# Values and phi(keys) turned by VectorE blocks and two DMA hops instead of TensorE transposes

## The chip, the cores and the metric

The kernel runs on one core of a Trainium2 chip. A core has five engines that run side by side: TensorE (PE in the profile; PEld is its weight load), VectorE (DVE), ScalarE (ACT), GpSimd (POOL) and SyncE (SP), which here issues most DMAs. Each engine takes its instructions in order and waits on semaphores for the others. The metric is device time in microseconds, the median of several runs.

## The reference: attention with a compressive memory, then an MLP

Input x is 2048 tokens by 1024. The first block normalises the rows, projects them to queries, keys and values of 32 heads of 32, and works in four segments of 512 tokens. Each segment has softmax attention inside it and a read of a memory M that earlier segments have written:

```python
phi = lambda t: jnp.where(t > 0, t + 1.0, jnp.exp(t))
for s in range(N):
    qs, ks, vs = q[:, :, s], k[:, :, s], v[:, :, s]
    p = _softmax(einsum("bhqd,bhkd->bhqk", qs, ks) * scale + mask)
    a_dot = einsum("bhqk,bhkd->bhqd", p, vs)
    num = einsum("bhld,bhde->bhle", phi(qs), M)
    den = einsum("bhld,bhd->bhl", phi(qs), z)[..., None] + 1e-6
    outs.append(g * num / den + (1.0 - g) * a_dot)
    M = M + einsum("bhld,bhle->bhde", phi(ks), vs)
    z = z + einsum("bhld->bhd", phi(ks))
```

The result is projected by wo and added to x; a layer norm, a dense layer to 3584, GELU and a dense layer back to 1024 follow, with a second residual. Everything is float32.

## The kernel before, in words

Float32 accuracy comes from splitting each factor into an upper half of the reduced type fp32r and the remainder, and from three products (upper by upper, upper by lower, lower by upper). `mm3` (L114 to L117) issues such a triple. The upper half is a copy, mostly by ScalarE, and the lower half a subtraction, by VectorE or GpSimd.

The tokens are worked in two halves of 1024. A half runs attention over two segments, then the output projection (`wo_first`, `wo_second`), then the MLP, whose two matrix products are built from shared partial sums. Only attention is touched.

Attention works in units. A unit is a group g of four heads (128 columns, eight groups) and one segment s of 512 tokens; a half has 16 units, the kernel 32. Two generators run interleaved, one step of each in turn, 24 steps a unit (counted over a unit, steps 0 to 7 project keys, 8 to 15 queries, 16 to 23 values):

- `dense` (L402) projects keys, queries and values of the unit, eight steps each (`kps`, `qps`, `vps`: 128 x 512 in PSUM, columns of the heads on the partitions, tokens along the row). The keys' and queries' halves are copied by SP into stacks `ks` and `qs` of 96 partitions (`stack`, 12 DMAs of 64 KB for each; five buffers, so a stack waits until the logits of an earlier head are done).
- `heads` runs softmax attention of the four heads of the unit before, one head per six steps, as a pipeline over three heads (`slot`, the list PLAN): logits `pqk`, exponential on ScalarE, normalisation `pr` on GpSimd (L557), transposes `ppt` of the weights on TensorE (L573), halves `pth` and `ptl`, products `po` with the values (L593).

Two tensors have to be turned, so that tokens lie on the partitions: the values, for `po` and for the memory update, and phi(keys) (`pk`, L369) for the memory update. phi(keys) is turned in segments 0 to 2 (24 units), the values in all 32.

- phi(keys): in step 1 of the value projection TensorE makes four transposes `pkn` (L453), ScalarE copies the upper half `pkh` (L455), and one step later VectorE subtracts for `pkl` (L457).
- Values: after the projection ScalarE copies `vps` to `vt` (L461). The generator `late` (L466) belongs to a unit but runs behind the next unit's steps, from step 2 of its key projection on. It begins with four transposes `vn` (L469) and the two halves of `vs` (L471, L472).

Then `late` lists small products, which go one by one into the places where `one_small` is called (before each `ppt` and most `po`): the memory read, 12 products `pm`, and the memory update, 12 products `pmm`, which need `vs`, `pkh` and `pkl`. The update of the state `MZ` follows (L497 on VectorE, L499 to L502 on GpSimd), and the next segment's unit copies its halves `mzh`, `mzl` on GpSimd in step 20 of its own. `pom` turns the memory output back (L516).

PSUM has three banks of the kind `d` (`ps_dense`), which projections, `pkn`, `vn`, `pm`, `pmm` and `pom` share. Within attention a scheduler fixes each engine's order before the run; the engines then follow that order whatever the real times are. The weights of the next group come as three DMAs `wr` of 512 KB (L326) and are split into `wh` and `wl` (L92).

Of the kernel before, what the change touches and what calls it, by code (L numbers as in the profile page):

```python
# [10 lines left out]
F32 = mybir.dt.float32  # L11
# [28 lines left out]
def raw(ap):  # L40
    return ap.bitcast(F32)


def build(tc, x, wq, wk, wv, wo, beta, w1, b1, w2, b2, out):
# [6 lines left out]
    def ps_dense(name):  # L51
        return psum.tile([P, 512], F32, tag="d", name=name, bufs=3)
# [29 lines left out]
    p1_dram = [dram.tile([P, 512], F32, name=f"p1_dram{j}") for j in range(FB // 2)]  # L82
    h_dram = [[dram.tile([S // P, P, FB // 4, P], F32, name=f"h_dram{i}{s}") for s in range(2)] for i in range(2)]

    acts = {}

    def split(pool, w, hi, lo, hi_eng="vector", lo_eng="gpsimd"):
# [256 lines left out]
    def attention(half, first):  # L344
# [4 lines left out]
        def tmp(name):  # L349
            return ab.tile([P, 512], F32, tag="tmp", name=name, bufs=5)  # L350

        def tmpr(name):
            return ab.tile([P, 512], F32R, tag="tmpr", name=name, bufs=6)

# [47 lines left out]
        def dense(g, sl, ws, u):  # L402
# [15 lines left out]
            for c in project(ws["q"], sl, "qps", qps):  # L418
                if c == 0:
                    u["ks"] = stack(kh, kl, "ks", (0, 1, 0))  # L420
                if c == 2 and s < 3:
                    zc = ab.tile([P, 64], F32, name="zc", bufs=2)[:, 0:1]
                    pk = phi_sum(kparts, "pk", zc)
                next(behind, None)
                yield
            qh, ql = tmpr("qh"), tmpr("ql")
# [6 lines left out]
            for c in project(ws["v"], sl, "vps", vps):  # L433
                if c == 0:
                    u["qs"] = stack(qh, ql, "qs", (0, 0, 1))
                if s > 0:
                    if c == 2:
                        pq = phi_sum(qparts, "pq")
                    if c == 4:
                        while small:  # L440
                            one_small()
                        pqh, pql = tmpr("pqh"), tmpr("pql")
                        mzh = ab.tile([P, 256], F32R, name="mzh", bufs=1)[:, 0:132]
                        mzl = ab.tile([P, 256], F32R, name="mzl", bufs=1)[:, 0:132]
                        nc.scalar.copy(pqh, pq)
                        nc.gpsimd.tensor_copy(mzh, MZ[:, g, :])
                        nc.gpsimd.tensor_tensor(mzl, MZ[:, g, :], raw(mzh), op=ALU.subtract)
                    if c == 5:
                        nc.gpsimd.tensor_tensor(pql, pq, raw(pqh), op=ALU.subtract)
                if c == 1 and s < 3:  # L450
                    pkn = ps_dense("pkn")
                    for i in range(4):
                        nc.tensor.transpose(pkn[:, i * P:(i + 1) * P], pk[:, i * P:(i + 1) * P], ident)  # L453
                    pkh, pkl = tmpr("pkh"), tmpr("pkl")
                    nc.scalar.copy(pkh, pkn)  # L455
                if c == 2 and s < 3:
                    nc.vector.tensor_tensor(pkl, pkn, raw(pkh), op=ALU.subtract)  # L457
                next(behind, None)
                yield
            vt = tmp("vt")  # L460
            nc.scalar.copy(vt, vps)  # L461
            vs = ab.tile([P, 16, 64], F32R, name="vs", bufs=2)
            u["vs"] = vs
            omt = u["omt"] = tmp("omt") if s > 0 else None

            def late():  # L466
                vn = ps_dense("vn")
                for c in range(4):
                    nc.tensor.transpose(vn[:, c * P:(c + 1) * P], vt[:, c * P:(c + 1) * P], ident)  # L469
                vn3 = vn.rearrange("p (a b) -> p a b", b=DH)  # L470
                nc.scalar.copy(vs[:, :, 0:32], vn3)  # L471
                nc.vector.tensor_tensor(vs[:, :, 32:64], vn3, raw(vs[:, :, 0:32]), op=ALU.subtract)  # L472
                yield
                if s > 0:
                    om = tmp("om")

                    def memory(i2, ps):
                        pm = ps.rearrange("p (a b) -> p a b", a=2)
                        rg = ab.tile([P, 2, 32], F32, name="rg", bufs=2)[:, :, 0:4]
                        nc.vector.scalar_tensor_tensor(  # L480
                            rg, pm[:, :, 128:132], DEN_EPS, bb[:, 4 * g:4 * g + 4].unsqueeze(1).to_broadcast([P, 2, 4]),
                            op0=ALU.add, op1=ALU.mult)
                        nc.vector.reciprocal(rg, rg)
                        nc.vector.tensor_tensor(
                            om[:, i2 * 256:(i2 + 1) * 256].rearrange("p (a h e) -> p a h e", a=2, h=4),
                            pm[:, :, 0:128].rearrange("p a (h e) -> p a h e", h=4),
                            rg.unsqueeze(3).to_broadcast([P, 2, 4, DH]), op=ALU.mult)

                    for i2 in range(2):
                        smalls("pm", [(lambda ps, ii=ii: ps[:, 256 * ii:256 * ii + 132],  # L490
                                       pqh[:, (2 * i2 + ii) * P:(2 * i2 + ii + 1) * P],
                                       pql[:, (2 * i2 + ii) * P:(2 * i2 + ii + 1) * P], mzh, mzl, True, True)
                                      for ii in range(2)], partial(memory, i2))
                left = len(small)
                if s < 3:
                    def update(pmm):
                        nc.vector.tensor_tensor(MZ[:, g, 0:P], pmm[:, 0:P], MZ[:, g, 0:P], op=ALU.add)  # L497
                        own = MZ[:, g, 0:P].rearrange("p (h e) -> p h e", h=4)
                        nc.gpsimd.tensor_tensor(own, own, hsel.unsqueeze(2).to_broadcast([P, 4, DH]), op=ALU.mult)  # L499
                        z = ZC[:, g:g + 1]  # L500
                        nc.gpsimd.tensor_scalar(z, z, zc, None, op0=ALU.add)
                        nc.gpsimd.tensor_scalar(MZ[:, g, 128:132], hsel, z, None, op0=ALU.mult)  # L502

                    smalls("pmm", [(lambda ps: ps[:, 0:P].rearrange("p (a b) -> p a b", a=4),
                                    pkh[:, c * P:(c + 1) * P], pkl[:, c * P:(c + 1) * P],
                                    vs[:, 4 * c:4 * c + 4, 0:32], vs[:, 4 * c:4 * c + 4, 32:64], c == 0, c == 3)
                                   for c in range(4)], update)
                total = len(small)
                while len(small) > total - left:
# [72 lines left out]
        def av(st, n):  # L582
# [3 lines left out]
            po = st["po"]  # L586
            for jk in (0, 1) if n == 0 else (3, 2):
                w = 512 - P * jk
                v = u["vs"][:, 4 * jk + j, :]
                for part in ("pth", "ptl"):  # L590
                    if (jk, part) != (3, "ptl"):
                        one_small()
                    nc.tensor.matmul(po[:, P * jk:], v, st[part][:, koff[jk]:koff[jk] + w],  # L593
                                     start=(jk, part) == (0, "pth"), stop=(jk, part) == (2, "ptl"))
# [849 lines left out]
```

## Time and profile before

| what | value |
|---|---|
| median of 3 runs | 2300.75 us (2300.48 to 2301.89) |
| the profiled execution: first to last instruction | 2296.2 us |
| between that span and the median | 4.55 us |
| instructions in the profile | 35279 |
| DMA in the profile | 355.36 MB, 155 GB/s on average |
| attention, half 0 | up to about 500 us |
| attention, half 1 | about 920 to 1380 us |

In the profile's rows a duration of a matmul includes its way through the array, so that rows overlap: the distance between starts tells what one costs. A row of a tile's view gives the line, engine, operation, the tiles, the count, and the shortest, median and longest duration. A timeline row gives the start in us, the duration in us, the engine, the line, the operation, the tile it writes and those it reads. SPq rows are SP issuing a DMA; a row of DMA issues ends with the median us from issue to landing.

### The profile page before, as it was taken

How to read it: one execution, taken by the hardware profiler on the slowest of the kernel's cores; microseconds unless marked ns; L12 is line 12 of the kernel's file. 1: busy time of each engine (PE TensorE's matmuls, PEld its weight loads, DVE VectorE, ACT ScalarE, POOL GpSimd, SP SyncE). 2: the span in 40 equal slices, each digit the busy share in tenths (PEclk: the TensorE clock that was granted, in tenths of full speed). 3: DMA queues.
4: the chain of work that ended last, by engine and by line, in shares of the span. 5: the costliest groups of instructions: out<-in, count | busy, mean ns of one | idle time of the engine just before them, and what ended most of it. 6: DMA issues, size and time to landing. Idle time of an engine off the chain costs nothing.

```text
span 2296.2 us, 35279 instructions
## 1 busy us (share of the span) xinstructions
PE 2270.4 (99%) x11769; PEld 1890.8 (82%) x11769; DVE 1540.3 (67%) x3173; ACT 1225.0 (53%) x2549; POOL 1092.4 (48%) x1134
## 2 busy tenths in 40 slices
PE   8999999999999999999999999999999999999999
PEld 6888888878888888888888887888888888888887
DVE  6777777776655565777777777565566766577563
ACT  6777777775453445777777776363344223322221
POOL 5545555555244442555555556253445554155430
PEclk9999999999999999999999999999999999999999
DMA  6333333345465654433333344466667976476762
GB/s 190 92 85 91 93 89 85 87 120 182 139 204 172 188 165 142 113 91 86 85 87 88 87 111 140 156 211 175 176 188 263 345 243 216 159 253 221 249 234 90
DMA packets 322719, 355.36 MB, mean 155 GB/s; under 512 B 26190, under 2 KB 218730, under 8 KB 322538
## 3 DMA queue, kind: packets, MB, share of 16 engines
q1 hardware_dynamic: 259370, 316.40, 45.4%
q10 hardware_dynamic: 63168, 36.71, 5.3%
q8 instruction: 93, 1.52, 0.3%
q14 instruction: 88, 0.72, 0.1%
HBM read 226.59 MB, written 76.09 MB: 132 GB/s over the span
## 4 chain that ended last, share of the span: by engine, by line
PE 91%; ACT 3%; POOL 2%; DVE 2%; issue 1%; DMA 1%; ACTq 0%; SPq 0%; POOLq 0%; DVEq 0%
PE po L1278 22%; PE bps L882 9%; PE cps L882 7%; PE dps L882 6%; PE po L593 6%; PE ppt L573 6%; PE pqk L541 3%; PE vps L116 2%; PE vps L115 2%; PE kps L115 2%; PE kps L116 2%; PE vps L117 2%; PE kps L117 2%; PE pwo L117 2%; PE pwo L116 2%; PE pwo L115 2%
## 5 line engine op out<-in xcount | busy, mean ns | idle before, releaser
L557 POOL TENSOR_SCALAR pr<-pr,nm,gate 128x128 f32<-128x128 f32 (+3 forms) x512 | 322.6, 639 | 345.9 <-DVE nm L554 260.0
L550 ACT ACTIVATE pr<-pr,mx 128x256 f32<-128x256 f32 (+3 forms) x512 | 287.6, 562 | 161.9 <-DVE mx L542 158.2
L580 DVE TENSOR_TENSOR ptl<-ppt,pth 128x512 fp32r<-128x512 f32 (+1 forms) x384 | 227.2, 599 | 86.2 <-ACT pth L575 82.0
L542 DVE CUSTOM_DVE_ANT_0 pr<-pqk,mask 128x256 f32<-128x256 f32 (+3 forms) x512 | 243.3, 484 | 46.5 <-PE pqk L541 43.7
L573 PE MATMUL ppt<-ident,pr 128*128 128x128 f32 x1280 | 223.6, 277 | 2.1 <-POOL pr L557 1.4
L575 ACT CAST pth<-ppt 128x512 fp32r<-128x512 f32 (+1 forms) x384 | 194.2, 517 | 39.0 <-PE ppt L573 33.1
L1288 DVE TENSOR_TENSOR c<-c,po 128x512 f32<-128x512 f32 x160 | 105.4, 683 | 143.1 <-PE po L1278 135.5
L573 PEld LDWEIGHTS ppt<-ident,pr 128*128 128x128 f32 x1280 | 164.6, 140 | 32.5 <-POOL pr L557 2.6
L541 PE MATMUL pqk<-ks,qs 96*128 96x256 f32 (+3 forms) x512 | 161.3, 315 | 0.0
L92 POOL TENSOR_TENSOR wl<-wr,wh 128x1024 fp32r<-128x1024 f32 x52 | 124.5, 2393 | 70.8 <-PE pqk L541 27.6
L593 PE MATMUL po<-pth,vs 128*64 128x512 f32 (+3 forms) x512 | 155.4, 326 | 0.3 <-ACT pth L575 0.2
L593 PE MATMUL po<-ptl,vs 128*64 128x512 f32 (+3 forms) x512 | 153.9, 310 | 1.3 <-DVE ptl L580 1.2
L1278 PE MATMUL po<-w2h,zh 128*128 128x512 f32 x378 | 121.1, 390 | 0.8 <-DVE zh L1218 0.4
L1135 POOL TENSOR_TENSOR w2r<-w2r 128x512 f32<-128x512 f32 x54 | 85.4, 1593 | 72.0 <-DVE c L1288 36.9
L541 PEld LDWEIGHTS pqk<-ks,qs 96*128 96x128 f32 x512 | 96.2, 188 | 21.5
L994 POOL TENSOR_TENSOR s<-r 128x512 f32<-128x512 f32 x28 | 43.6, 1559 | 143.4 <-DVE sa L1010 87.1
L882 PE MATMUL bps<-zh,sb 128*128 128x512 f32 x336 | 111.0, 391 | 0.0
L882 PE MATMUL bps<-zh,sa 128*128 128x512 f32 x336 | 110.8, 390 | 0.0
L115 PE MATMUL vps<-yh,wh 128*128 128x512 f32 x256 | 109.4, 427 | 0.9 <-DVE MZ L497 0.9
L115 PE MATMUL kps<-yh,wh 128*128 128x512 f32 (+1 forms) x264 | 110.1, 417 | 0.0
L115 PE MATMUL qps<-yh,wh 128*128 128x512 f32 x256 | 106.8, 417 | 0.0
L1278 PE MATMUL po<-w2h,hl 128*128 128x512 f32 x322 | 103.2, 390 | 0.5 <-POOL hl L1218 0.3
(241 smaller groups left out, 6657.1 us busy)
## 6 DMA issues: line engine op xcount, KB each, us to landing
hr<-h_dram SPq DMA_DIRECT2D x112, 448.0 KB, 5.4
w2r<-in_B_w SPq DMA_DIRECT2D x122, 256.0 KB, 4.4
r<-in_B_w SPq DMA_DIRECT2D x56, 512.0 KB, 4.5
h_dram<-ht ACTq DMA_DIRECT2D x84, 256.0 KB, 3.7
ks<-kh SPq DMA_DIRECT2D x256, 64.0 KB, 2.0
qs<-qh SPq DMA_DIRECT2D x256, 64.0 KB, 2.0
wr<-in_A_wo SPq DMA_DIRECT2D x32, 512.0 KB, 4.0
wx<-in_B_w SPq DMA_DIRECT2D x56, 256.0 KB, 3.5
```

Of the source, the lines that this page charges most:

```text
L115: nc.tensor.matmul(ps, ah, bh, start=first, stop=False)
L116: nc.tensor.matmul(ps, ah, bl, start=False, stop=False)
L541: nc.tensor.matmul(pqk[:, :n], u["qs"][j][:, i * P:(i + 1) * P], u["ks"][j][:, 0:n], start=True, stop=True)
L542: nc.vector.tensor_tensor_reduce(out=st["pr"][:, offs[i]:offs[i] + n], in0=pqk[:, :n], in1=mask[:, 512 - n:512], op0=ALU.add, op1=ALU.min, ...
L550: nc.scalar.activation(pi, pi, AF.Exp, bias=mx[:, i:i + 1], scale=-1.0, accum_out=mx[:, 4 + i:5 + i])
L557: nc.gpsimd.tensor_scalar(pi, pi, nm[:, 4 + k:5 + k], gate[:, 1, 4 * g + j:4 * g + j + 1], op0=ALU.mult, op1=ALU.mult)
L573: nc.tensor.transpose(ppt[:, o:o + P], pr[:, offs[i] + jk * P:offs[i] + (jk + 1) * P], ident)
L575: acts["pth"] = n, nc.scalar.copy(pth[:, base:base + w], ppt[:, :w])
L580: nc.vector.tensor_tensor(o, x0, x1, op=ALU.subtract)
L593: nc.tensor.matmul(po[:, P * jk:], v, st[part][:, koff[jk]:koff[jk] + w], start=(jk, part) == (0, "pth"), stop=(jk, part) == (2, "ptl"))
L882: nc.tensor.matmul(ps, x_[:, c, :], y_[:, c, :], start=first and c == 0 and n == 0, stop=last and c == 3 and n == 2, skip_group_check=True)
L1278: nc.tensor.matmul(ps, x_[:, k], y_[k], start=opens and k == 0 and i == 0, stop=closes and k == self.KP - 1 and i == 2, skip_group_check=True)
```

## The change

Neither tensor is turned by TensorE any more. A new function `turned` does it in two hops. VectorE transposes each 32 x 32 block of the 128 x 512 tile in place of its block (a single instruction; for the values it reads PSUM). SP stores the result to one of four scratch buffers in memory, and four loads, one for each quarter of the 128 target partitions, bring it back with the blocks in the places that a full transpose gives them, but for the order along the row: heads outermost, then the four blocks of 128 tokens. The later readers are rewritten for that order (`vk`, and `4 * j + jk` in `av`).

- phi(keys): `turned` is called in step 3 of the query projection, the copy to `pkh` moves from step 1 to step 2 of the value projection and reads SBUF, and the subtraction for `pkl` moves from VectorE in step 2 to GpSimd in step 3.
- Values: `turned` reads `vps` itself, so the copy `vt` goes. In `late` the memory products are listed first; the upper half of `vs` is made six steps later, the lower half one step after it, and the update products are listed two steps after that.
- The scratch tiles `scr` in SBUF take the place of two tiles that hold weights of the output projection after attention.

```diff
+    turn_dram = [dram.tile([P, 512], F32, name=f"turn_dram{k}") for k in range(4)]
...
+        scr = [acts["zt"].tile([P, 4, 512], F32, tag=f"t{x_}3", name=f"sc{x_}") for x_ in "hl"]
+
+        def turned(src, to, at):
+            mid = at
+            nc.vector.transpose(mid.rearrange("p (c k d) -> p c k d", c=4, k=4), src.rearrange("p (k c d) -> p c k d", c=4, k=4))
+            d = turn_dram[acts.get("turned", 0) % len(turn_dram)]
+            acts["turned"] = acts.get("turned", 0) + 1
+            nc.sync.dma_start(d, mid)
+            for c in range(4):
+                nc.sync.dma_start(to[32 * c:32 * c + 32].rearrange("j (h x) -> j h x", h=4),
+                                  d[:, c * P:(c + 1) * P].rearrange("(h j) x -> j h x", h=4))
...
+                if c == 3 and s < 3:
+                    kn = scr[1][:, 2 + sl]
+                    turned(pk, kn, scr[1][:, sl])
...
-                if c == 1 and s < 3:
-                    pkn = ps_dense("pkn")
-                    for i in range(4):
-                        nc.tensor.transpose(pkn[:, i * P:(i + 1) * P], pk[:, i * P:(i + 1) * P], ident)
+                if c == 2 and s < 3:
                     pkh, pkl = tmpr("pkh"), tmpr("pkl")
-                    nc.scalar.copy(pkh, pkn)
-                if c == 2 and s < 3:
-                    nc.vector.tensor_tensor(pkl, pkn, raw(pkh), op=ALU.subtract)
+                    pkn = kn.rearrange("p (h k d) -> p k h d", h=4, k=4)
+                    pk4 = [x_.rearrange("p (k h d) -> p k h d", h=4, k=4) for x_ in (pkh, pkl)]
+                    nc.scalar.copy(pk4[0], pkn)
+                if c == 3 and s < 3:
+                    nc.gpsimd.tensor_tensor(pk4[1], pkn, raw(pk4[0]), op=ALU.subtract)
...
-            vt = tmp("vt")
-            nc.scalar.copy(vt, vps)
+            vn = scr[0][:, 2 + sl]
+            turned(vps, vn, scr[0][:, sl])
...
             def late():
-                vn = ps_dense("vn")
-                for c in range(4):
-                    nc.tensor.transpose(vn[:, c * P:(c + 1) * P], vt[:, c * P:(c + 1) * P], ident)
-                vn3 = vn.rearrange("p (a b) -> p a b", b=DH)
-                nc.scalar.copy(vs[:, :, 0:32], vn3)
-                nc.vector.tensor_tensor(vs[:, :, 32:64], vn3, raw(vs[:, :, 0:32]), op=ALU.subtract)
-                yield
                 if s > 0:
...
+                for _ in range(6):
+                    yield
+                vn3 = vn.rearrange("p (a b) -> p a b", b=DH)
+                nc.scalar.copy(vs[:, :, 0:32], vn3)
+                yield
+                nc.vector.tensor_tensor(vs[:, :, 32:64], vn3, raw(vs[:, :, 0:32]), op=ALU.subtract)
+                vk = vs.rearrange("p (h k) e -> p k h e", h=4)
+                yield
+                yield
                 left = len(small)
...
-                                    vs[:, 4 * c:4 * c + 4, 0:32], vs[:, 4 * c:4 * c + 4, 32:64], c == 0, c == 3)
+                                    vk[:, c, :, 0:32], vk[:, c, :, 32:64], c == 0, c == 3)
...
-                v = u["vs"][:, 4 * jk + j, :]
+                v = u["vs"][:, 4 * j + jk, :]
```

## The prediction

> **What bounds the kernel now.** I read the engine totals first, then the chain that ended last, then the waits of TensorE, then the busy time of the two attention stages.
>
> ```profile
> span 2296.2 us, 35279 instructions
> PE 2270.4 (99%) x11769; PEld 1890.8 (82%) x11769; DVE 1540.3 (67%) x3173; ACT 1225.0 (53%) x2549; POOL 1092.4 (48%) x1134
> PE 91%; ACT 3%; POOL 2%; DVE 2%; issue 1%; DMA 1%; ACTq 0%; SPq 0%; POOLq 0%; DVEq 0%
> ```
> ```profile
> sum 915.00, PE 910.00 PEld 768.24 DVE 686.99 ACT 669.90 POOL 500.48; mean PE 455.00 PEld 384.12 DVE 343.49 ACT 334.95 POOL 250.24
> ```
> ```profile
> PE ppt L573 <- POOL pr L557: 1.4, 4, 0.5
> ```
>
> The chain is TensorE for 91% of the span. The second fence sums two stretches, 45 to 500 us and 920 to 1380 us, which are the attention of the two halves, the only place that the change touches: TensorE is busy for 910.0 of 915.0 us, VectorE for 75%, ScalarE 73%, GpSimd 55%. The last line is a row of TensorE's waits (total, times, longest): even its normalised weights `pr` are late only four times. So every microsecond of TensorE issue that goes is a microsecond of the result, until some other engine's chain becomes late.
>
> **The change, part by part.** What goes and what is replaced:
>
> ```profile
> L453 PE MATMUL pkn<-ident,pk x96: 270/272/273, 31.5 to 1333.3; 128*128 128x128 f32 x96
> L469 PE MATMUL vn<-ident,vt x128: 271/272/329, 40.6 to 1380.8; 128*128 128x128 f32 x128
> L457 DVE TENSOR_TENSOR pkl<-pkn,pkh x24: 678/680/691, 34.3 to 1335.4; 128x512 fp32r<-128x512 f32 x24
> ```
>
> 224 transposes leave TensorE: 24 groups of four for the keys, 32 for the values. Their 272 ns each are no measure, because they overlap; what counts is how far they push apart the starts around them.
>
> ```profile
> 209.73 0.39 PE L117 MATMUL qps<-yh,wl 128*128 128x512 f32 x1
> 209.96 0.34 PE L541 MATMUL pqk<-ks,qs 96*128 96x384 f32 x1
> 210.13 0.60 PE L573 MATMUL ppt<-ident,pr 128*128 128x128 f32 x4
> ...
> 213.46 0.39 PE L117 MATMUL vps<-yh,wl 128*128 128x512 f32 x1
> 213.69 0.60 PE L453 MATMUL pkn<-ident,pk 128*128 128x128 f32 x4
> ...
> 214.58 0.40 PE L116 MATMUL vps<-yl,wh 128*128 128x512 f32 x1
> ...
> 220.91 0.39 PE L117 MATMUL vps<-yh,wl 128*128 128x512 f32 x1
> 221.14 0.38 PE L573 MATMUL ppt<-ident,pr 128*128 128x128 f32 x2
> 221.28 0.48 PE L115 MATMUL kps<-yh,wh 128*128 128x512 f32 x1
> 221.60 0.39 PE L116 MATMUL kps<-yl,wh 128*128 128x512 f32 x1
> ...
> 224.21 0.39 PE L117 MATMUL kps<-yh,wl 128*128 128x512 f32 x1
> 224.44 0.60 PE L469 MATMUL vn<-ident,vt 128*128 128x128 f32 x4
> 224.79 0.43 PE L541 MATMUL pqk<-ks,qs 96*128 96x384 f32 x1
> 225.06 0.60 PE L573 MATMUL ppt<-ident,pr 128*128 128x128 f32 x4
> ...
> 251.19 0.48 PE L115 MATMUL kps<-yh,wh 128*128 128x512 f32 x1
> ```
>
> A unit (one head group, one segment) lasts 251.19 - 221.28 = 29.9 us, from its first key product to that of the next; it has 24 steps of about 1.25 us.
>
> - Values: from L117 over one pqk of 384 to ppt takes 225.06 - 224.21 = 0.85 us with `vn` in between, and 210.13 - 209.73 = 0.40 without. 0.45 us a group, 32 x 0.45 = 14.4 us.
> - Keys: from L117 over two ppt and L115 to L116 takes 214.58 - 213.46 = 1.12 us with `pkn`, 221.60 - 220.91 = 0.69 without. 0.43 us, 24 x 0.43 = 10.3 us.
>
> Together **-24.7 us** on the bounding engine. The Trainium skill, VectorE: DVE Perf Modes, The three transpose paths, gives 390 ns for one 128x128 on TensorE in bf16 and 311 ns for VectorE, which turns 32x32 blocks alone, and its Rules for kernel authors keep a 128x128 transpose on TensorE where PSUM will do; that rule speaks against this change. By its price TensorE would shed an estimated 224 x 0.39 = 87 us; these rows show 0.11 us of issue for each.
>
> Small products. The 12 update products `pmm` of a unit move from steps 4 to 8 into steps 11 to 14 of the next unit, behind the halves of the values; the memory products `pm` take their old places. In the built order of the changed kernel they stand among ppt and po as before. Four of them cost:
>
> ```profile
> 215.85 0.22 PE L541 MATMUL pqk<-ks,qs 96*128 96x128 f32 x1
> 216.71 0.39 PE L115 MATMUL vps<-yh,wh 128*128 128x512 f32 x1
> ...
> 227.25 0.39 PE L117 MATMUL kps<-yh,wl 128*128 128x512 f32 x1
> 228.16 0.48 PE L115 MATMUL kps<-yh,wh 128*128 128x512 f32 x1
> ...
> 230.80 0.22 PE L541 MATMUL pqk<-ks,qs 96*128 96x128 f32 x1
> 231.97 0.40 PE L115 MATMUL qps<-yh,wh 128*128 128x512 f32 x1
> ```
>
> Among transposes 0.91 us against the 0.58 (224.21 to 224.79) of a projection and four transposes alone: 0.08 each. Among four po 1.17 against 0.86: 0.08 each. The move is worth 0; with 288 of them and some 0.005 us of uncertainty, 1.5 us to either side.
>
> Other engines, a unit. ScalarE loses the copy `vt`. VectorE loses `pkl` (0.68) and gets two block transposes of 128x512, one from PSUM. No such operation is in the trace. The nearest row is the subtraction above at 0.68 us; half of it and twice of it are the bounds, and I take 0.7, since size and engine are the same: two of them less `pkl` are +0.7 us of 29.9, from 75% to some 78%, beside TensorE.
>
> The transfers are the real question. Each turn is one 256 KB store to memory and, after it has landed, four 64 KB loads, all issued by SP, in order, between the `ks`/`qs` copies.
>
> ```profile
> ks<-kh SPq DMA_DIRECT2D x256, 64.0 KB, 2.0
> wr<-in_A_wv SPq DMA_DIRECT2D x16, 512.0 KB, 4.4
> o_dram<-ot SPq DMA_DIRECT2D x28, 256.0 KB, 2.3
> ```
> ```profile
> 205.62 0.53 SPq L609 DMA_DIRECT2D o_dram<-ot  x1
> 212.04 0.51 SPq L377 DMA_DIRECT2D ks<-kh  x1
> ```
> ```profile
> 214.37 0.60 ACT L455 CAST pkh<-pkn 128x512 fp32r<-128x512 f32 x1
> 260.94 0.59 ACT L413 CAST kh<-kps 128x512 fp32r<-128x512 f32 x1 [1.14 <-PE kps L117]
> ```
> ```profile
> 255.50 0.37 SPq L326 DMA_DIRECT2D wr<-in_A_wq  x1
> ```
>
> A turn takes, from the store's issue: 2.3 us to land (as o_dram), four issues of 0.6 (0.51 to 0.53 in these rows, and a little between), 2.0 for the last to land: 2.3 + 2.4 + 2.0 = 6.7 us. Bounds: 5.5 us (2.0 + 3 x 0.51 + 2.0, both hops as quick as a `ks` copy) and 10.6 us (4.4 + 3 x 0.6 + 4.4, both hops as slow as the weight load `wr`). I take the middle one, since o_dram has the store's size and form and `ks` the loads' size.
>
> - Keys: in the built order the store stands behind o_dram, at 206.2 us on this unit's clock; it ends at 212.9. The consumer `pkh` is moved one step, from 214.37 to 214.9 at the earliest. 2.0 us of slack; SP is free from 206.2 to 212.04, so `ks` behind it loses up to 0.5 us, and those wait for a buffer anyway. At the bound of 10.6 us ScalarE stands 1.9 us, the exponentials queue behind `pkh`, `pkl` on GpSimd behind it, and `pr` behind that.
> - Values: the projection ends at 221.3, the block transpose some 1 us later, the store near 222.8, the loads land at 229.5. The consumer `vs` stands next to `kh`, 10 us behind the start of the unit, that is 231.3 or later. 1.8 us of slack. In a unit whose successor loads weights, SP puts two weight loads between store and loads; the second waits for GpSimd until 255.50, so the four loads go at 255.9 and land near 260.3, while `kh` is at 260.94. Slack 0.5 us, gone if anything slips.
>
> GpSimd in the units with weights is where I expect the first wait:
>
> ```profile
> 242.78 2.40 POOL L92 TENSOR_TENSOR wl<-wr,wh 128x1024 fp32r<-128x1024 f32 x1 [1.12 <-PE pqk L541]
> 245.16 1.42 POOL L557 TENSOR_SCALAR pr<-pr,nm,gate 128x384 f32<-128x384 f32 x2
> ```
> ```profile
> 247.50 0.60 PE L573 MATMUL ppt<-ident,pr 128*128 128x128 f32 x4
> ```
>
> GpSimd gets `pkl`: 1.2 us, half of what `wl` takes for twice the columns, 55% to 58% of a unit, between two `pr`. `pr` ends at 246.58, and ppt wants it at 247.50: 0.92 us. TensorE, with the key group gone, wants it 0.43 us sooner. The memory state's update, four operations of at most 132 columns (by the 1.42 us that two `pr` of 896 columns take, 0.3 each, 1.2 us), now falls just ahead of `wl`, because `pmm` ends in step 14 instead of step 8, and starts `wl` 0.2 to 0.5 us late. That uses up the slack: I take 0.2 us in the 16 units of this kind, 3 us, and 2 us more for the two ends of attention, where the scratch for the turned tiles is the home of two weight tiles of the output projection, which now wait for the last `vs`. **+5 us**, bounds 0 and 15.
>
> Sum against the profiled execution: 2296.2 - 24.7 + 5 = 2276.5 us of span. The median of the runs, 2300.75, lies 4.55 above that span, so 2281 us.
>
> **The rivals.**
> 1. Some cover is thin: a landing is late by part of a microsecond in most turns, and TensorE pays 0.25 us for each of 56: +14 more, 2295 us. For it: the 0.5 us slack above. Against: ScalarE idles about 1 us before `kh` (quoted), which absorbs it.
> 2. The other side: the landing takes the place of the transposes. A turn of 10.6 us makes ScalarE stand at `pkh` and `vs`, in order, with the exponentials behind it. It decides from 24.7 / 56 = 0.44 us of TensorE per turn on; at 0.9 us for each it is 2300.75 - 24.7 + 50 = 2326 us. For it: two hops, 512-byte rows, one in-order queue. Against: the rows of 2.0 and 2.3 us.
> 3. SP's own issue becomes the bound: 34 copies a unit at 0.6 us are 20.4 us, with two landings awaited 25 us, against 29.9. It decides above 29.9; at 2 us over in 30 units it is 2300.75 - 24.7 + 60 = 2336 us. The Trainium skill, Perfetto Trace Analysis, What "DMA-bound" means, names an issuing queue that is solid with transfers as such a bound; here it would not be solid.
> 4. It doesn't do what it says: the transposes sat in gaps that TensorE has anyway, and 2300 us stays. Against: the pushed-apart starts above, and 5.0 us of idle in 915.
>
> **How the numbers follow.** The forecast (covers hold; 2274, with no wait at all and 1.5 us from the small products, to 2291, with 15 of waits) has 0.63; rival 1 has 0.14, of which 0.13 still faster and 0.01 the same; rival 4 has 0.05; rival 2 has 0.16 and rival 3 has 0.02, both slower. 0.2% (4.6 us) is about what a measurement of this kernel can tell from no change. Faster 0.76, same 0.06, slower 0.18. The range goes from two below the forecast's own lower end (2272; some of the 5.0 us of idle may go too) up past rivals 1 and 4 to the beginning of rival 2 (2304); what lies above has less than 0.2.
>
> **What would show it.** TensorE's matmuls fall by 224; its busy time in the attention stretches shrinks by about 25 us and its idle grows by less than 8. A wait of ScalarE for the turned tiles, at `vs` in units with weight loads, is short. Turns land within 6 to 8 us of the store's issue; a landing of the four loads above 3 us, ScalarE waits for them of over 1 us in most units, or ppt waits on `pr` summing to tens of microseconds would make this wrong.

## The result

The changed kernel takes **2364.32 us** (median of 4 runs, 2362.57 to 2367.69) against 2301.32 (4 runs, 2300.48 to 2303.18): ratio 1.0275, 95% interval 1.0261 to 1.0290. It is 63 us slower; the prediction was 20 us faster, and its range ended at 2304. The profiled execution has a span of 2360.6 us, 64.4 more than before.

The head of the changed kernel's page (span; busy time of each engine; the chain that ended last):

```profile
span 2360.6 us, 35257 instructions
PE 2276.5 (96%) x11545; PEld 1874.8 (79%) x11545; DVE 1566.2 (66%) x3205; ACT 1206.7 (51%) x2517; POOL 1134.5 (48%) x1158
PE 73%; DVE 11%; DMA 5%; ACT 4%; POOL 4%; issue 3%; SPq 1%; DVEq 0%; ACTq 0%; POOLq 0%
```

TensorE has 11769 - 11545 = 224 matmuls fewer, as foreseen. But it carries 73% of the chain, not 91%: VectorE has 11% and DMA 5%. The two attention stretches, 45 to 510 and 930 to 1410 us here, summed, and TensorE's waits in the first 1500 us (what waits, for what; total, times, longest):

```profile
sum 945.00, PE 891.01 PEld 733.49 DVE 693.74 ACT 635.05 POOL 516.57; mean PE 445.51 PEld 366.75 DVE 346.87 ACT 317.52 POOL 258.29
```
```profile
PE ppt L591 <- DVE ptl L598: 31.4, 26, 2.4
PE ppt L591 <- POOL pr L575: 9.2, 16, 1.2
...
PE pm L409 <- POOL pql L466: 5.8, 3, 3.3
PE po L611 <- DVE ptl L598: 4.3, 3, 3.5
PE pqk L559 <- DVE mx L560: 4.1, 21, 0.4
PE pwo L117 <- POOL zl L93: 2.8, 2, 1.7
```

In these stretches TensorE idles for 54 us of 945, where it was 5 of 915. They end a little before attention does here: the output projection begins at 526.8 and 1436.0 us, before the change at 501.0 and 1374.0. Cut there, attention grew by 58 us (45 to 501 and 920 to 1374 before, 45 to 527 and 950 to 1436 after); TensorE's idle time in it grew from 5.0 to 59.3 us, and its busy time did not shrink (905.0 and 908.7 us), in part because some of it runs at a lower clock, as the last section shows. The largest wait is new: the transposes of the weights, `ppt`, wait for VectorE to read the tile before last (`ptl`), 26 times. VectorE is busy 73% of these stretches, and 75% before: the average shows nothing.

To place all of the time, I took the distance of each matmul's start from the one before it and subtracted the median distance that the same three neighbours have in the trace before. What is left is waiting (and slower running); its sum by place, in us, up to 1500 us:

| where | before | after |
|---|---|---|
| step 11 (26 units: all but the first two and last of a half) | 0.2 | 34.7 |
| steps 7 and 8 of these | 2.4 | 16.3 |
| step 20 of these | 0.1 | 9.8 |
| their other steps | 3.3 | 7.1 |
| start of attention: lead-in, units 0, 1, 16, 17 | 9.4 | 23.8 |
| units 15 and 31, with the output projection's begin | 10.2 | 23.4 |
| sum | 25.6 | 115.2 |

89.6 us of waits came, and 64.4 us of span: the difference, 25.2 us, is the work that left TensorE. The remainder is good to some 10 us only, since neighbours that the trace before does not have need a substitute. The length of single steps shows the work directly. Step 17, where `pkn` stood, is 0.43 to 0.44 us shorter than before in these 26 units where the keys are turned, and 0.00 in segment 3, where they never were; step 2, where `vn` stood, is 0.43 us shorter where no `pm` has moved into it. That is 24 x 0.43 + 32 x 0.43 = 24.1 us. So the predicted 24.7 us are there, and waits took them more than three times over.

**Step 11 of one unit.** VectorE, then TensorE:

```profile
212.52 0.68 DVE L508 TENSOR_TENSOR vs<-sch,vs 128x512 fp32r<-128x512 f32 x1
...
213.34 0.68 DVE L428 TENSOR_TENSOR kl<-kps,kh 128x512 fp32r<-128x512 f32 x1
...
215.17 0.69 DVE L383 SCALAR_TENSOR_TENSOR pk<-e,r 128x512 f32<-128x512 f32 x1 [0.56 <-ACT r L378]
...
215.91 0.71 DVE L358 STREAM_TRANSPOSE scl<-pk 128x512 f32<-128x512 f32 x1
216.54 0.65 DVE L560 CUSTOM_DVE_ANT_0 pr<-pqk,mask 128x512 f32<-128x512 f32 x1
...
217.13 0.69 DVE L598 TENSOR_TENSOR ptl<-ppt,pth 128x512 fp32r<-128x512 f32 x1
```
```profile
216.51 0.22 PE L409 MATMUL pmm<-vs,pkh 128*128 128x128 f32 x1
217.96 0.30 PE L591 MATMUL ppt<-ident,pr 128*128 128x128 f32 x1 [1.24 <-DVE ptl L598]
```

`ppt` has two PSUM banks. The third group of a head, in step 11, needs the bank of the first, and that is free once `ptl` has read it. The same stretch of steps 8 to 11 holds the halves of the keys, `pk` and the masks; into this stretch the change puts both halves of `vs` and the block transpose, and the fixed order has them ahead of `ptl`. On ScalarE the upper half of `vs`, at times with its wait for the loads, stands ahead of `pth` in the same way:

```profile
211.79 0.62 ACT L506 CAST vs<-sch 128x512 fp32r<-128x512 f32 x1 [0.91 <-DMA sch<-turn_dram]
...
215.62 0.59 ACT L593 CAST pth<-ppt 128x512 fp32r<-128x512 f32 x1
```

### The profile page after: what moved, and what is told of

Read it like the earlier page. It is cut to its first block, busy times and chain, and to the rows that moved or that the text cites. A ratio compares the mean times of both kernels' runs of the same rounds, so it can differ in the third digit from the quotient of the medians.

```text
span 2360.6 us, 35257 instructions
## 1 busy us (share of the span) xinstructions
PE 2276.5 (96%) x11545; PEld 1874.8 (79%) x11545; DVE 1566.2 (66%) x3205; ACT 1206.7 (51%) x2517; POOL 1134.5 (48%) x1158
## 4 chain that ended last, share of the span: by engine, by line
PE 73%; DVE 11%; DMA 5%; ACT 4%; POOL 4%; issue 3%; SPq 1%; DVEq 0%; ACTq 0%; POOLq 0%
PE po L1296 20%; PE bps L900 9%; PE cps L900 6%; PE dps L900 6%; PE po L611 4%; PE ppt L591 4%; PE pwo L117 2%; PE pwo L118 2%; PE pwo L116 2%; DVE ptl L598 2%; DVE pr L560 2%; PE pqk L559 2%; PE vps L116 2%; PE vps L117 2%; PE vps L118 2%
## 5 line engine op out<-in xcount | busy, mean ns | idle before, releaser
L575 POOL TENSOR_SCALAR pr<-pr,nm,gate 128x128 f32<-128x128 f32 (+3 forms) x512 | 329.5, 653 | 363.7 <-DVE nm L572 306.7
L591 PE MATMUL ppt<-ident,pr 128*128 128x128 f32 x1280 | 227.1, 280 | 42.6 <-DVE ptl L598 31.4
L593 ACT CAST pth<-ppt 128x512 fp32r<-128x512 f32 (+1 forms) x384 | 186.7, 513 | 63.0 <-PE ppt L591 58.6
L118 PE MATMUL qps<-yh,wl 128*128 128x512 f32 x256 | 101.8, 398 | 1.7 <-POOL wl L93 1.7
```

The costliest lines, as they stand in the source:

```text
L118: acts["mm"] = nc.tensor.matmul(ps, al, bh, start=False, stop=last)
L575: nc.gpsimd.tensor_scalar(pi, pi, nm[:, 4 + k:5 + k], gate[:, 1, 4 * g + j:4 * g + j + 1], op0=ALU.mult, op1=ALU.mult)
L591: nc.tensor.transpose(ppt[:, o:o + P], pr[:, offs[i] + jk * P:offs[i] + (jk + 1) * P], ident)
L593: acts["pth"] = n, nc.scalar.copy(pth[:, base:base + w], ppt[:, :w])
```

## The experiments

Theory **Q** is that queue: what the change puts ahead of `ptl` on VectorE and ScalarE. The rival **L** is rival 2 of the prediction: the loads land late and ScalarE stands. All runs had the kernel before beside them, at 2301.2 to 2302.2 us.

### One tensor at a time, and the places alone

**Keys alone** turned by VectorE and DMA, values as before:

```diff
-            vn = scr[0][:, 2 + sl]
-            turned(vps, vn, scr[0][:, sl])
+            vt = tmp("vt")
+            nc.scalar.copy(vt, vps)
...
+                vn = ps_dense("vn")
+                for c in range(4):
+                    nc.tensor.transpose(...)   # and the halves, first in late, as before
```

> Keys alone turned by VectorE and DMA; the values turned by TensorE, with the halves of vs at their old place. Theory Q (in steps 8 to 11 VectorE and ScalarE are full, and what the change adds there, the halves of vs and the block transpose of pk, stands ahead of ptl of the first weights, whose PSUM bank TensorE wants in step 11): only the block transpose is left of it, 0.7 us against some 0.2 us of slack, 24 x 0.5 = 12 us lost, some 8 us lost on GpSimd (pkl ahead of pr), 10 us won on TensorE: about 2311 us. Theory L (the late landing of the turned values, and the exponentials behind it on ScalarE): no turned values, so 2301 - 10 + 8 = 2299 us.

Measured 2305.67 us, ratio 1.0018 (1.0009 to 1.0028). Neither forecast came: step 11 has 0.2 us of waits where Q had 12, and the time is 7 us above L's.

**Values alone**: the keys as before, the values as after the change.

```diff
-                if c == 3 and s < 3:
-                    kn = scr[1][:, 2 + sl]
-                    turned(pk, kn, scr[1][:, sl])
...
+                if c == 1 and s < 3:
+                    pkn = ps_dense("pkn")
+                    for i in range(4):
+                        nc.tensor.transpose(...)   # pkh by ScalarE, pkl by VectorE, as before
```

> Values alone turned by VectorE and DMA; keys by TensorE as before. Q: the halves of vs still stand ahead of ptl, the block transpose of pk does not: 24 x 0.7 = 17 us less than the changed kernel, 10 us more on TensorE, 8 us less on GpSimd: about 2350 us, with a wait of some 0.6 us in step 11 of every unit. L: the loads of the values are as late as in the changed kernel: 2364 + 10 - 8 = 2366 us.

Measured 2333.71 us, ratio 1.0136 (1.0121 to 1.0151): 16 us below Q's forecast and 32 below L's.

**The places alone**: TensorE turns both, but `vn` and its halves stand behind six more steps, and `pmm` behind those, as in the changed kernel:

```diff
                 for _ in range(6):
                     yield
+                vn = ps_dense("vn")
+                for c in range(4):
+                    nc.tensor.transpose(vn[:, c * P:(c + 1) * P], vt[:, c * P:(c + 1) * P], ident)
                 vn3 = vn.rearrange("p (a b) -> p a b", b=DH)
                 nc.scalar.copy(vs[:, :, 0:32], vn3)
```

> Both turned by TensorE as before, but at the changed kernel's places: the values' transposes and halves in steps 8 and 9 of the next unit, the update products in steps 11 to 14. Q: the halves of vs are ahead of ptl, 0.5 to 0.9 us lost in 30 units: 2316 to 2328 us. L, or any theory by which the turn itself costs the time: 2301 us within 3.

Measured 2317.14 us, ratio 1.0065 (1.0049 to 1.0081): 16 us with no turn and no transfer. L alone falls. But the place of the 16 is not where Q had it: step 11 has 2.6 us of waits here, steps 7 and 8 have 8.3 and step 20 has 8.5. With the keys alone step 11 has 0.2 us of waits, with the values alone 16.9, and there ScalarE waits 21.2 us for the values' loads. The two together lose more than their sum: +4.5 and +32.5 against +63 us.

### The order

Three instructions of the changed kernel are held back by an order constraint without a semaphore: the block transpose of `pk` behind `ptl` of step 9, the upper half of `vs` behind `pth`, the lower half behind that `ptl`. The halves are also listed two steps later, so the loads get two steps more to land, and the update products come two steps later too.

```diff
-            nc.vector.transpose(mid..., src...)
+            behind_of(nc.vector.transpose(mid..., src...), ("sub", 0))
...
-                for _ in range(6):
+                for _ in range(8):
                     yield
-                nc.scalar.copy(vs[:, :, 0:32], vn3)
+                behind_of(nc.scalar.copy(vs[:, :, 0:32], vn3), ("pth", 0))
                 yield
-                nc.vector.tensor_tensor(vs[:, :, 32:64], ...)
+                behind_of(nc.vector.tensor_tensor(vs[:, :, 32:64], ...), ("sub", 0))
```

> The changed kernel, with three instructions held back in their engine's order: the block transpose of pk behind ptl of the first weights in step 9, the upper half of vs behind pth, the lower half behind that ptl, all else as it is. Q: the wait of TensorE in step 11 (28 units x 1.3 us = 36 us) goes, 2364 - 36 = 2328 us, and some 10 us more if the smaller waits in steps 7 and 8 have the same cause. L: the landing has two steps more, so at most the 14 us that ScalarE waited for it: 2350 us or more, with the wait of step 11 still there.

Measured 2332.79 us, ratio 1.0135 (1.0118 to 1.0152), 31.5 us less than the changed kernel with the same instructions on every engine. Its waits of `ppt`, and the place on VectorE's timeline:

```profile
PE ppt L598 <- DVE ptl L605: 2.2, 4, 0.7
```
```profile
210.90 0.92 DVE L390 SCALAR_TENSOR_TENSOR pk<-e,r 128x512 f32<-128x512 f32 x1 [0.34 <-ACT r L385]
...
211.75 0.68 DVE L605 TENSOR_TENSOR ptl<-ppt,pth 128x512 fp32r<-128x512 f32 x1
212.35 0.69 DVE L365 STREAM_TRANSPOSE scl<-pk 128x512 f32<-128x512 f32 x1
```

31.4 us of this wait have become 2.2, and step 11 has 1.0 us in the 26 units instead of 34.7. The waits of steps 7 and 8 did not go (19.9 us): they have another cause. Two things went that the order does not explain: ScalarE's waits for the values' loads (14.0 us in the changed kernel, none here), and 8.9 of the 9.8 us in step 20, because the update of `MZ`, two steps later, now falls behind `wl`. So this run does not test the order by itself. The block transpose held back alone does, with nothing else moved:

```diff
-            nc.vector.transpose(mid..., src...)
+            behind_of(nc.vector.transpose(mid..., src...), ("sub", 0))
```

> The changed kernel with one instruction held back: the block transpose of pk behind ptl of the first weights in step 9; the halves of vs stay where the change has them. Q (what stands ahead of ptl on VectorE): the transpose is half of what is ahead, 0.7 us in 23 units, 16 us: about 2348 us, with a wait of 0.3 to 0.9 us left in step 11. If the halves of vs alone make the wait: 2364 us. If the transpose alone: 2333 us, as with both held back.

Measured 2346.75 us, ratio 1.0192 (1.0178 to 1.0206): 17.6 us of the 31.5 are the block transpose's place, with 20.3 us left in step 11 and 9.9 in step 20. The other 13.9 us belong to the halves of `vs`, their place and the two steps together; these runs do not separate the two.

### The way through memory

As the run on the order, without store and loads, so that the halves are made from the block-turned tile itself:

```diff
-            d = turn_dram[...]
-            nc.sync.dma_start(d, mid)
-            for c in range(4):
-                nc.sync.dma_start(to[32 * c:32 * c + 32]..., d[...]...)
```

> Three instructions held back in the order as in the run before, and the way through memory left out: no store and no loads, the halves are copied from the blocks that VectorE turned, so values and phi(keys) stand in wrong places and the output is not the reference's. If what is left of the loss (2333 us, 57 us of TensorE waits more than before the change, some 30 of them in units 1, 2, 15, 17, 18 and 31) comes from the transfers (landings, SP's issue, weight loads behind them): 2333 - 30 = 2303 us or less. If it comes from work on VectorE and GpSimd (the order, their shared access to SBUF, the late update products): within 8 us of 2333.

Measured 2317.18 us, ratio 1.0061 (1.0045 to 1.0076): 15.6 us less, between the two expectations. So the transfers cost something, but only half of the rest. By places, 9.2 us of it lie at the starts of attention (20.6 to 11.4 us). There SP is the likely reason, though no run took it apart: in the changed kernel it issues from 931.8 us on with hardly a pause, until the weights of the values' projection have their turn:

```profile
951.09 0.53 SPq L361 DMA_DIRECT2D turn_dram<-sch  x1
951.83 0.40 SPq L327 DMA_DIRECT2D wr<-in_A_wv  x1
```

### The keys' own loss

Keys alone should win 10 us and lost 4. First, `pkl` back on VectorE:

```diff
-                    nc.gpsimd.tensor_tensor(pk4[1], pkn, raw(pk4[0]), op=ALU.subtract)
+                    nc.vector.tensor_tensor(pk4[1], pkn, raw(pk4[0]), op=ALU.subtract)
```

> Keys alone turned by VectorE and DMA, pkl back on VectorE instead of GpSimd. The version with pkl on GpSimd took 2305.7 us although TensorE has 10 us less to do. If GpSimd's pkl is what it loses (a wait of 2.9 us in unit 17 for pql, small ones in units with weights): 2301 - 10 + 5 = 2296 us. If the turn's transfers or the block transpose lose it: 2304 to 2307 us.

Measured 2305.03 us, ratio 1.0013 (1.0004 to 1.0022): `pkl` on GpSimd was not it. Then also the block transpose behind `ptl`, and the first unit of each half by TensorE:

```diff
-                if c == 3 and s < 3:
+                if c == 3 and s < 3 and not (g == 0 and sl == 0):
...
+                if c == 1 and s < 3 and g == 0 and sl == 0:
+                    pkn = ps_dense("pkn")          # transposes and pkh as before
```

> Keys alone turned by VectorE and DMA, pkl on VectorE, the block transpose behind ptl of the first weights, and the first unit of each half turned by TensorE as before (2 of 24 units). If SP's issue and the loads at the start of a half are what keys alone lose, with GpSimd: 2301 - 9.5 + 1 = 2293 us. If it is the block transpose's time on VectorE: as with pkl on VectorE alone, within 2 us.

Measured 2303.95 us, ratio 1.0007 (0.9998 to 1.0015). Unit 17's waits are as before the change (1.8 us, 7.2 with the run above), so the start was a part. The held-back transpose took it away again: step 13 has 8.2 us of waits, 3.0 with the run above. The medians are 1 us apart, which this measurement cannot tell from none.

### Shared tiles, late products, GpSimd

The run on the order, with the turned tiles in the buffers of `tmp`:

```diff
-            vn = scr[0][:, 2 + sl]
-            turned(vps, vn, scr[0][:, sl])
+            vn = tmp("sch")
+            turned(vps, vn, vn)            # and the same for the keys
```

> As the run with three instructions held back (2333 us), but the turned tiles stand in buffers of the five that tmp has, and the loads write back into the tile that was stored; the tiles of the output projection's weights are left alone. If their shared home is what TensorE waits for at the two ends of attention (units 15 and 31: 23.0 us of waits in that run, 10.2 before the change): 2333 - 13 = 2320 us. If the ends wait for something else, or five buffers of tmp are too few: 2330 us or more.

Measured 2335.96 us, ratio 1.0144 (1.0128 to 1.0160): no gain. Units 15 and 31 have 19.2 us instead of 23.0, step 13 has 18.3 instead of 12.8. The shared home is a small part of the ends.

The kernel before, with `pmm` late alone:

```diff
                 left = len(small)          # kernel before, L494
+                for _ in range(8):         # ahead of this line
+                    yield
```

> The kernel before, both turned by TensorE with the halves at their old places; only the twelve update products of a unit are listed eight steps later. The run with everything at the changed kernel's places but turned by TensorE lost 16 us. If the late products make the late update of MZ on GpSimd and with it the wait of 0.7 us in step 20 of 7 units: 2301 + 5 = 2306 us, and the halves of vs lose the other 11. If the prediction's 0 for moved products holds: 2301 us within 2.

Measured 2307.68 us, ratio 1.0028 (1.0017 to 1.0039). Six us for the late products alone. In its profile step 20 has 8.5 us of waits, 1.4 in each of the six odd units of the first half that the table counts: the update of `MZ` falls ahead of the weight split `wl` on GpSimd. What TensorE waits for there is VectorE:

```profile
PE pqk L543 <- DVE mx L544: 7.7, 8, 1.1
```

In unit 5 `pq`, a VectorE instruction with two inputs in SBUF, now runs beside `wl` and takes 1.53 us instead of 0.96, and the mask that frees the bank for `pqk` stands behind it. In the changed kernel the late `wl` reaches TensorE by another way: `pr` stands behind it on GpSimd, and `ppt` waits for `pr` twice in each of these units (0.67 and 0.42 us in unit 5).

On the run with own tiles, the lower half of `vs` by GpSimd:

```diff
-                behind_of(nc.vector.tensor_tensor(vs[:, :, 32:64], ...), ("sub", 0))
+                nc.gpsimd.tensor_tensor(vs[:, :, 32:64], ...)
```

> As the run with own tiles and three instructions held back, and the lower half of vs is subtracted by GpSimd instead of VectorE. If VectorE's time is still what TensorE waits for (the subtraction takes 0.69 us, and 1.25 to 2.4 where GpSimd works beside it; waits of 0.4 to 0.6 us in step 13, as much in steps 7 and 8): 28 x 0.4 = 11 us less than with own tiles. If GpSimd's 1.3 us come between pr and ppt instead: the same or more.

Measured 2352.48 us, ratio 1.0219 (1.0204 to 1.0235): 16.5 us worse than with own tiles. GpSimd needs 1.29 us for the subtraction, and the waits of `po` for `ptl` rose from 16.2 to 24.8 us.

Keys alone with `pkl` on VectorE, the first unit of each half by TensorE, the block transpose not held back, and `kn = tmp("scl")`:

> Keys alone turned by VectorE and DMA, pkl on VectorE, the first unit of each half by TensorE, the turned tile in a buffer of tmp, turned in place. The same with the shared home and the transpose held back took 2304 us, TensorE 9.5 us less work than before, 2.6 us more waits in unit 15. If the home made those: 2299 to 2301 us, about as before. If the transpose and pkl on VectorE make the waits in all units: 2303 to 2305 us.

Measured 2302.03 us, ratio 1.0004 (0.9995 to 1.0012): the same as before the change. No version of turned keys beats the kernel before.

### The memory products

The change lists `pm` one step earlier, since `vn` and a step went from ahead of it. In this run they are back:

```diff
             def late():
+                yield
                 if s > 0:
...
-                for _ in range(8):
+                for _ in range(7):
```

> As the run with three instructions held back (2333 us), and the memory products pm are listed one step later, where they stood before the change. If their place makes the waits in steps 7 and 8 (1.05 us in even units, 0.4 in odd ones, 20 us over 28 units, of which 2 were there before): 2333 - 18 = 2315 us. If the prediction's 0 for moved products holds: 2333 us.

Measured 2327.12 us, ratio 1.0111 (1.0094 to 1.0127). Steps 7 and 8 have 2.9 us, as before the change, instead of 19.9. The place of `pm` was the cause; but only 5.7 us came out, because the next wait was close behind. Step 13 went from 12.8 to 20.0 us, and there `po` now waits for the lower half of `vs` itself:

```profile
PE po L619 <- DVE vs L516: 13.7, 14, 1.3
```

The same without store and loads:

> The same without the way through memory (the output is not the reference's: values and phi(keys) stand in wrong places). 2317 us before pm was moved back. If steps 7 and 8 were pm's place: 2317 - 18 = 2299 us, and what is left against 2276 (2301 less TensorE's 25) is the subtraction of vs beside GpSimd in step 13 and the ends of attention. If not: 2317 us.

Measured 2307.83 us, ratio 1.0024 (1.0015 to 1.0034): 9.4 us by `pm`, and 19.3 by the transfers against the run before this. Of the 61.7 us of waits that are left, 36 more than before the change, 20.9 are in step 13 and 22.9 in units 15 and 31.

Values alone, with the two halves of `vs` held back and `pm` back:

> Values alone turned, keys by TensorE as before, the halves of vs held back behind pth and ptl, pm back at its old place. 2334 us without the two last. If order and pm were all that values lost beside the transfers: 2334 - 13 (step 11) - 15 (steps 7 and 8) = 2306 us, still not below 2301. If the subtraction of vs beside GpSimd is a loss of its own in step 13: 2312 us or more.

Measured 2309.95 us, ratio 1.0034 (1.0020 to 1.0047): 24 us better than values alone unmended, between the two expectations, and still not below the kernel before.

## Why the prediction was wrong, point by point

- **-24.7 us on TensorE**: right. The shorter steps 2 and 17 give 24.1 us.
- **VectorE "from 75% to some 78%, beside TensorE", costed at nothing**: this step failed, and the largest new wait, 31.4 us of `ppt` on `ptl`, comes from it. The block transpose has the size that I took:

```profile
L358 DVE STREAM_TRANSPOSE sch<-vps x32: 690/706/718, 38.1 to 1436.1; 128x512 f32<-128x512 f32 x32
```
```profile
L358 DVE STREAM_TRANSPOSE scl<-pk x24: 690/711/714, 30.1 to 1383.4; 128x512 f32<-128x512 f32 x24
```

  What was wrong is the cover. A share of 75% over a unit says nothing on steps 8 to 11, where before the change `ptl` ended at 204.86 us and `ppt` followed at 205.08:

```profile
204.17 0.69 DVE L580 TENSOR_TENSOR ptl<-ppt,pth 128x512 fp32r<-128x512 f32 x1 [0.47 <-ACT pth L575]
```
```profile
205.08 0.30 PE L573 MATMUL ppt<-ident,pr 128*128 128x128 f32 x1
```

  I looked up where the moved `vs` halves stand for the sake of their loads, and not what is queued behind them. Shown: the block transpose's place alone costs 17.6 us; with the halves of `vs` held back and two steps later it is 31.5 us. With the keys alone turned the same transpose at the same place makes no wait in step 11 (0.2 us): the cover held one more instruction, and not that one together with the halves of `vs`.
- **The lower half of `vs`** was costed as moved, not as changed. Its source went from PSUM to SBUF. The same line before, with TensorE at the changed places, and after:

```profile
L472 DVE TENSOR_TENSOR vs<-vn,vs x32: 682/686/692, 41.9 to 1383.2; 128x512 fp32r<-128x512 f32 x32
```
```profile
L509 DVE TENSOR_TENSOR vs<-vn,vs x32: 677/680/690, 48.2 to 1409.1; 128x512 fp32r<-128x512 f32 x32
```
```profile
L508 DVE TENSOR_TENSOR vs<-sch,vs x32: 677/693/2370, 58.4 to 1448.3; 128x512 fp32r<-128x512 f32 x32
```

  In the changed kernel 16 of the 32 overlap an instruction of GpSimd and take 1.63 us on average, the other 16 take 0.68 to 0.69; VectorE loses 15.0 us by it, inside the burst. How much of that TensorE pays no run took apart.
- **Small products, 0 +- 1.5**: wrong. I priced their issue on TensorE, 0.08 us at both places that I read. But `pm` has VectorE's `om` behind it and `pmm` GpSimd's update: `pm` one step early costs 5.7 to 9.4 us, `pmm` late 6.
- **The turn of 6.7 us, with slack**: right for the keys, too short for the values. The issues of DMAs of the changed kernel (KB each, median us from issue to landing):

```profile
turn_dram<-sch SPq DMA_DIRECT2D x32, 256.0 KB, 2.3
sch<-turn_dram SPq DMA_DIRECT2D x128, 64.0 KB, 3.8
turn_dram<-scl SPq DMA_DIRECT2D x24, 256.0 KB, 2.5
scl<-turn_dram SPq DMA_DIRECT2D x96, 64.0 KB, 2.1
```

  By the same sum the keys' turn takes 2.5 + 2.4 + 2.1 = 7.0 us and the values' 2.3 + 2.4 + 3.8 = 8.5; the term of 2.0 for their loads was mis-sized by 1.8 us, which is all the slack there was. Counted one by one from the store's issue, by the landings in the trace, the 32 turns of the values take 5.2 to 13.6 us, 8.4 in the median. ScalarE waited for them 12 times:

```profile
  DMA sch<-turn_dram: 14.0, 12
```

  Costing the transfers at nothing was wrong by 15.6 to 19.3 us. Of the rivals' times the 2336 us of rival 3 (SP's issue) and the 2326 us of rival 2 (the landing) lay nearest, but both are about the transfers, and with no transfer at all the loss is smaller by no more than those 15.6 to 19.3 us: less than the 25 us that TensorE saves.
- **GpSimd in units with weights, 3 us**: the mechanism (the state's update ahead of `wl`) was right, the size was not: step 20 has 9.7 us more, 1.5 in each odd unit of the first half and next to nothing in the second. `pkl`, which I counted in, showed no part: with keys alone, `pkl` on GpSimd and the products at their old place, step 20 has 0.2 us. **The two ends, 2 us**: 13.2; the shared tiles explain about 4 of it.
- **Thin covers, one behind the other**: with one wait mended, the next took part of the gain. Step 11 lost 34 us of waits and step 13 got 10 (2.3 to 12.8); steps 7 and 8 lost 17 and step 13 got 7 more. One run built on the other, they lead from 2364 us by 31.5 (held back, two steps later), 5.7 (`pm`) and 19.3 (transfers) to 2308 us. What keeps that 31 us above 2302 - 25 = 2277 is by place step 13 and the ends; step 13 is `po` behind the lower half of `vs`, the ends were not taken apart further, so this part of the cause stays open.
- **The signs that I listed**: the 224 matmuls went. The busy time did not shrink by 25 us, the idle time grew by 54 and not by less than 8, the values' loads took 3.8 us and not less than 3, and 17 of their 32 turns took more than 8. ScalarE's waits (12 of 32) and `ppt` on `pr` (9.2 us) stayed below my bounds. The wait that cost most, `ppt` on `ptl`, was not among the signs.

## What to carry to other kernels

An engine's share of busy time is no cover. Before a step is put on an engine "beside" the bounding one, read that engine's timeline at the place, and find what is behind the new instruction and which buffer it frees: here a transpose of 0.7 us ahead of one PSUM read in each of 24 units cost 17.6 us beside the other moved instructions, and made no wait there without them. A moved instruction brings along what hangs on it, on every engine; its own issue is the least of it. And where a kernel has several thin covers, a saving on the bounding engine is taken by whichever is next, so a mended wait gives back less than it measured.

## What the runs showed of the hardware

**A subtraction on VectorE with both inputs in SBUF can stand still beside a subtraction on GpSimd.** The longest case, VectorE and GpSimd:

```profile
1028.03 2.37 DVE L508 TENSOR_TENSOR vs<-sch,vs 128x512 fp32r<-128x512 f32 x1
```
```profile
1027.45 2.40 POOL L93 TENSOR_TENSOR wl<-wr,wh 128x1024 fp32r<-128x1024 f32 x1 [1.65 <-PE ppt L591]
```

GpSimd ends at 1029.85, VectorE at 1030.40, 0.55 us later, so it did little until then. With one input in PSUM the same subtraction took 0.69 us at most in 64 cases, 50 of them beside GpSimd. Of the 16 cases beside GpSimd in the changed kernel, the 11 beside `wl` take 1.44 to 2.37 us and the one beside `ol`, also a subtraction, 1.66; the four beside `pr` or the update of `MZ` alone take 0.68 to 0.96. The Trainium skill, SBUF — State Buffer, Who interferes with whom, says that such an instruction contends with one of GpSimd that reads SBUF. The traces agree for GpSimd's subtractions; beside `pr`, which reads SBUF too, they show 0.27 us at most. The figure for this kernel is 15 us of VectorE's time.

**A wait on TensorE costs more than its length.** Windows of the changed kernel around unit 17's wait of 3.3 us (columns: busy us of PE, PEld, DVE, ACT, POOL, then the granted clock, DMA share, GB/s):

```profile
951.50:955.00 3.50, 0.18 (x3) 0.06 (x1) 0.64 (x4) 0.99 (x4) 3.50 (x5) 0.90 0.78 232
955.00:958.00 3.00, 3.00 (x13) 2.83 (x14) 1.78 (x6) 1.56 (x4) 1.62 (x3) 0.50 0.04 13
958.00:961.00 3.00, 3.00 (x10) 2.31 (x10) 2.42 (x8) 1.76 (x5) 1.41 (x2) 0.50 0.00 0
```

The clock falls to half for some 6 us after the wait, and the starts there are 2 to 3 us further apart in all. In the kernel before the granted clock is 1.00 in every stretch from 45 to 1480 us. Over the whole execution its mean is 0.993 here and 1.000 before; if it is half wherever it is not full, that is an estimated 2 x 0.007 x 2360.6 = 33 us at half rate and some 16 us lost, which the table counts among the waits. The Trainium skill, TensorE: Matmul & The Clock Gate, What's actually happening, gives half rate after an idle window of some 3.4 us. Here a wait of 2.4 us was enough (TensorE was busy 1.29 us of the 3.60 up to 998.6), which is less than that window:

```profile
998.60:1002.40 3.80, 3.67 (x13) 3.16 (x14) 2.28 (x6) 1.81 (x6) 2.67 (x3) 0.55 0.49 145
```
